# Four instead of five plain experts in a one-core attention–MoE–FFN kernel, with the extra VectorE work tied to the side product's remainder

## The chip, the cores and the metric

The kernel runs on one core of one Trainium2 chip. The metric is the device time of one execution in microseconds. The five engines run their own instruction streams: TensorE (PE), VectorE (DVE), ScalarE (ACT), GpSimd (POOL), and SyncE (SP), which here issues the DMAs. An instruction waits for others through semaphores, and everything behind it on its own engine waits with it.

## The reference

Three layers follow each other. Attention takes the 32 largest scores of each row (2 batches, 8 heads, 576 rows, head size 64). Its output is x, 1152 rows of 512. The mixture of experts and the last layer are

```python
logits = x @ w_gate
P = np.exp(logits - logits.max())
for _ in range(8):
    P /= P.sum(1, keepdims=True) + 1e-09
    P /= P.sum(0, keepdims=True) + 1e-09
    P *= N / E
for e in range(E):                       # E = 8, F = 1024
    h = np.maximum(x @ w1[e], 0.0)
    out += P[:, e:e + 1] * (h @ w2[e])

h = out @ w_in                           # 512 x 2048
g = h * np.tanh(np.log1p(np.exp(h)))     # h itself above 20
result = g @ w_out                       # 2048 x 512
```

Every product is made to float32 accuracy from pairs of rounded numbers (a high part, and a low part that is the remainder), three matmuls for one. The last layer's weights come as the bits of float64.

## The kernel before

**Stages.** The 1152 rows are nine tiles of 128. The experts run in three chunks of rows: tiles 0 and 1, tiles 2 and 3 (both beside attention), and tiles 4 to 8, which is 640 rows, from about 559 to 994 us. Then comes the last layer ("d" in names), in two units of four and five tiles, to the end at 1196 us. This case is about the third chunk ("c2") and its seam to the last layer.

**Plain experts.** The weights of an expert come in eight pieces of 128 hidden columns. Experts 0 to PLAIN - 1 run piece by piece (`ffn_pass`). A piece has 24 first-layer matmuls (L805) and 15 of the second layer (L679). ACT writes the high part of the activation (`hh`, L633) and DVE the remainder (`hl`, L634).

**Seven products.** The other experts take two pieces at a time (`pair_pass`): the first layer of the pair is a 2x2 block product, done with seven products instead of eight (42 matmuls of 320 columns at L711). The banks `run` and `alt` (two of them in all) and one side bank `hs` take them in the order 11, side product 12, s2, s3 and s1, 22, s4; second-layer matmuls of the pair before stand in between, as groups of 6 and 9. DVE's part of a pair is written in `total` and `Relu.first`: `hs` becomes a total (L729) and gives a remainder (L634); `c` becomes a total (L729) and gives one; `run` gives one; `h` becomes a total and gives one. PE's s4 waits for the `c` total, because it writes the bank that the total reads, and the next pair's product 11 waits for the remainder of `run` for the same reason.

**Weights.** `load_pair` makes the weight sums on POOL (L569 to L573), ACT rounds each (`wh`, L542), and POOL subtracts (`wl`, L546). For the third chunk the raw pieces come from the weights; for "d" they come from a DRAM copy `w` that the kernel itself has made (next paragraph), into tiles `wraw_d` and `wrawb_d`.

**Work that fills the third chunk.** On DVE: 32 *doubles*, each a 128x512 block of float64 weights turned into float32 by one ACT square and six DVE operations (L954, L957 to L961), loaded by SP into `cx` and stored by SP (L962) from `cb` to `w`; 32 *rows*, in which a spilled second-layer output is read back and added (L826); and 24 *lefts* (L618 add or subtract, L619 cast, L620 subtract), the operand sums for seven products in the last layer's first unit. On POOL: 32 *sums*, the same three lines for the operand of the third chunk. The buffers of the doubles live in pool `cp`; when the doubles are done (`conv.close()`), pool `x2q`, which holds `wraw_d` and `wrawb_d`, takes the same memory.

**What sets the order.** PE's order is that of the program. On the other engines a priority by stream decides, except where `after(a, b)` says that a comes behind b. `pace` hangs doubles and rows behind the newest remainder `live["hl"]`, at rates in pieces (`DOUBLES`, `FILL_FROM`); `follow` gives lefts a credit and hangs one behind its second argument for each whole credit. In the loop over the third chunk's yields, `TURN_FROM`, `PAIRS_FROM` and `TURNS` say at which of them a tile of the finished output is transposed (`x2t`, L985), which the lefts need.

```python
pieces += 1 if pieces < PLAIN * EP else 2 / 3
pace(pieces)
if i >= TURN_FROM and (i - PAIRS_FROM) % 8 in TURNS:
    next(first_rows, None)
```

## Time and profile before

| | us |
|---|---|
| median of 3 runs (lowest to highest) | 1195.77 (1195.69 to 1196.48) |
| the profiled execution | 1198.0 |
| its span, first to last instruction | 1196.1 |
| PE busy | 1150.1 (96%) |
| DVE, ACT, POOL busy | 926.4, 712.8, 704.3 |

The span is the profiler's, of one execution, from the first instruction to the last. Busy time is the time in which an engine had an instruction in work, and an engine that is waited for can be far from fully busy. The mean granted TensorE clock is 0.994 of full speed.

### The profile page before, as it was taken

To read this page: it belongs to the slowest core of one execution; us is meant where nothing else is said; L and a number is where in the kernel's file an instruction comes from. 1 tells how busy PE (TensorE), PEld (TensorE's weight loads), DVE (VectorE), ACT (ScalarE), POOL (GpSimd) and SP (SyncE) were. 2 spreads that over 40 slices of the span, in tenths; PEclk is the share of its full clock that TensorE was granted. 3 is DMA by queue.
4 is the path that set the end of the run, shared out by engine and by line. 5 is a ranking of instruction groups with operands and counts; after the bars stand their busy time and mean duration, and the time that the engine had idled before them with its cause. 6 is when DMAs were issued, how large, how long until landed. Compare 5 with 4: busy or idle time off the path is not lost.

```text
span 1196.1 us, 21441 instructions
## 1 busy us (share of the span) xinstructions
PE 1150.1 (96%) x7251; PEld 1025.3 (86%) x7251; DVE 926.4 (77%) x1943; ACT 712.8 (60%) x1454; POOL 704.3 (59%) x607
## 2 busy tenths in 40 slices
PE   3788999999999999999999999999999999999998
PEld 2566888898888999889999999998898989889997
DVE  7999999999999999943578888777666457886442
ACT  5877777777777777754233333333455546767653
POOL 6544877888777787762223343433665576787651
PEclk9998999999999999999999999999999999999999
DMA  8358777657565677754257776766454332233201
GB/s 254 106 180 280 237 258 232 187 162 226 177 214 169 214 235 231 242 174 158 81 175 246 247 256 222 268 209 229 164 177 141 125 114 80 97 107 115 96 29 45
DMA packets 121967, 214.08 MB, mean 179 GB/s; under 512 B 16000, under 2 KB 26496, under 8 KB 121856
## 3 DMA queue, kind: packets, MB, share of 16 engines
q1 hardware_dynamic: 120560, 211.52, 54.5%
q8 instruction: 57, 0.93, 0.3%
q10 hardware_dynamic: 1296, 1.18, 0.3%
q14 instruction: 54, 0.44, 0.1%
HBM read 174.11 MB, written 38.54 MB: 178 GB/s over the span
## 4 chain that ended last, share of the span: by engine, by line
PE 87%; DVE 3%; DMA 1%; ACT 1%; issue 1%; POOL 0%; SPq 0%; ACTq 0%; POOLq 0%
PE y_c2e L679 17%; PE h_c2e L805 11%; PE y_d L679 8%; PE h_c1e L805 8%; PE y_c1e L679 8%; PE h_c0e L805 6%; PE y_c0e L679 6%; PE h_d L711 6%; PE h_c2e L711 5%; PE pv L358 3%; PE tr L335 2%; PE sc L236 2%; PE pv L365 1%; PE hs_d L711 1%; PE hs_c2e L711 1%
## 5 line engine op out<-in xcount | busy, mean ns | idle before, releaser
L546 POOL TENSOR_TENSOR wl_c1e<-wraw_c1e,wh_c1e 128x512 fp32r<-128x512 f32 x128 | 171.2, 1348 | 60.2 <-ACT wh_c1e L542 56.9
L546 POOL TENSOR_TENSOR wl_c0e<-wraw_c0e,wh_c0e 128x512 fp32r<-128x512 f32 x112 | 148.3, 1337 | 51.1 <-ACT wh_c0e L542 44.1
L264 DVE MAX8 top<-w 128x8 f32<-128x576 f32 x216 | 158.5, 748 | 1.0
L546 POOL TENSOR_TENSOR wl_c2e<-wraw_c2e,wh_c2e 128x512 fp32r<-128x512 f32 x40 | 53.2, 1330 | 171.6 <-ACT wh_c2e L542 163.7
L542 ACT ACTIVATE wh_c2e<-wraw_c2e 128x512 fp32r<-128x512 f32 x80 | 50.6, 632 | 143.6 <-PE y_c2e L679 76.9
L542 ACT ACTIVATE wh_c1e<-wraw_c1e 128x512 fp32r<-128x512 f32 x128 | 80.5, 629 | 47.3 <-PE y_c1e L679 22.1
L271 DVE MATCH_REPLACE8 w<-top,w 128x576 f32<-128x576 f32 x144 | 106.6, 741 | 0.0
L805 PE MATMUL h_c2e<-xh,wh_c2e 128*128 128x256 f32 (+1 forms) x320 | 98.7, 308 | 0.6 <-DVE hl_c2e L634 0.6
L805 PE MATMUL h_c2e<-xl,wh_c2e 128*128 128x256 f32 (+1 forms) x320 | 98.2, 307 | 0.0
L805 PE MATMUL h_c2e<-xh,wl_c2e 128*128 128x256 f32 (+1 forms) x320 | 98.1, 307 | 0.0
L542 ACT ACTIVATE wh_c0e<-wraw_c0e 128x512 fp32r<-128x512 f32 x112 | 70.4, 629 | 46.1 <-PE y_c0e L679 15.6
L634 DVE SCALAR_TENSOR_TENSOR hl_c2e<-h_c2e,hh_c2e 128x256 fp32r<-128x256 f32 (+1 forms) x104 | 50.6, 487 | 53.8 <-ACT hh_c2e L633 53.6
L236 PE MATMUL sc<-ks,q 128*128 128x288 f32 x320 | 66.0, 338 | 23.6 <-POOL ks L168 5.5
L236 PEld LDWEIGHTS sc<-ks,q 128*128 128x128 f32 x320 | 53.1, 211 | 34.1 <-ACT early L249 7.4
L679 PE MATMUL y_c2e<-wh_c2e,hl_c2e 128*128 128x512 f32 x200 | 78.7, 394 | 0.0
L679 PE MATMUL y_c2e<-wl_c2e,hh_c2e 128*128 128x512 f32 x200 | 78.4, 392 | 0.0
L679 PE MATMUL y_c2e<-wh_c2e,hh_c2e 128*128 128x512 f32 x200 | 78.4, 392 | 0.0
L805 PE MATMUL h_c1e<-xh,wh_c1e 128*128 128x256 f32 (+1 forms) x256 | 76.4, 298 | 0.0
L665 DVE TENSOR_TENSOR hl_d<-mg_d,hh_d 128x256 fp32r<-128x256 f32 (+1 forms) x64 | 50.5, 796 | 32.4 <-ACT hh_d L664 32.0
L805 PE MATMUL h_c1e<-xh,wl_c1e 128*128 128x256 f32 (+1 forms) x256 | 73.3, 286 | 0.0
L805 PE MATMUL h_c1e<-xl,wh_c1e 128*128 128x256 f32 (+1 forms) x256 | 73.2, 286 | 0.0
L805 PE MATMUL h_c0e<-xh,wh_c0e 128*128 128x256 f32 x224 | 66.7, 298 | 1.1 <-DVE hl_c0e L634 0.9
(532 smaller groups left out, 3963.0 us busy)
## 6 DMA issues: line engine op xcount, KB each, us to landing
wraw_c1e<-in_wst_dram SPq DMA_DIRECT2D x128, 256.0 KB, 3.1
wraw_c0e<-in_wst_dram SPq DMA_DIRECT2D x112, 256.0 KB, 3.2
wraw_c2e<-in_wst_dram SPq DMA_DIRECT2D x80, 256.0 KB, 3.3
cx<-in_w_dram SPq DMA_DIRECT2D x32, 512.0 KB, 5.0
yd<-ysp SPq DMA_DIRECT2D x32, 256.0 KB, 3.6
low<-wl_c1e SPq DMA_DIRECT2D x32, 256.0 KB, 2.7
yb<-yd SPq DMA_DIRECT2D x32, 256.0 KB, 3.6
wl_c2e<-low SPq DMA_DIRECT2D x32, 256.0 KB, 3.8
```

The costliest lines, as they stand in the source:

```text
L236: nc.tensor.matmul(halves[half], q[:, h % HG, :], ks[b, h][:, half * HS : (half + 1) * HS], start=(i == 0), stop=(i == len(terms) - 1),)
L264: top8 = nc.vector.max(g, src)
L271: nc.vector.match_replace(w, g, src, NEG)
L335: nc.tensor.transpose(tr[:, c, :], em[:, j * D + c * P :][:, :P], ident)
L358: nc.tensor.matmul(pv[i * D : (i + 1) * D, pair, c0:c1], vmain[b, pair][:, i, c, :], live["at", i][:, c, c0:c1], start=(c == 0), stop=False,)
L542: live["rounded"] = nc.scalar.activation(hi, raw, AF.Copy)
L546: eng.tensor_sub(lo, raw, hi)
L634: live["hl"] = nc.vector.scalar_tensor_tensor(l, ps, 0.0, h, op0=ALU.max, op1=ALU.subtract)
L665: follow(LEFT_RATE, nc.vector.tensor_sub(l, g, h))
L679: nc.tensor.matmul(y, h[:, j * P : (j + 1) * P], w, start=(start and k == 0), stop=(stop and k == len(products) - 1))
L711: nc.tensor.matmul(bank, a[:, cols], b[:, c, :], start=(start and c + k == 0), stop=(c == 1 and k == 2), skip_group_check=not start,)
L805: nc.tensor.matmul(ps, w[:, c * P : (c + 1) * P], x[:, c, c0 : c0 + m], start=(k == 0), stop=(k == 3 * NC - 1),)
```

## The change

One expert more (expert 4) runs by seven products: `PLAIN` is 4. The yields are counted anew (`PAIRS_FROM`, `TURN_FROM`), and the transposes are at two of three places (`TURNS[:2]`). The paces of rows, doubles and sums become tables of a start and a rate. In the experts by seven products the doubles and the lefts no longer hang behind whatever remainder came last. They hang behind the remainder of the side product (`live["lead"]`), in every pair but an expert's first, 2.7 lefts and one double for each such pair; `follow` is gone from `Relu` and, in the third chunk, from the totals. The combine of the last second-layer outputs is ordered behind a remainder (`put_last`).

```diff
--- before.py
+++ after.py
@@ -48,10 +48,10 @@
 EARLY_FROM, EARLY_STEPS = 5, 9
 HOLD, RATE = 8, 0.25
 ALONE, ALONE_RATE = 1, 3.4
-FILL_FROM = 9
-PLAIN = 5
-PAIRS_FROM, TURN_FROM = 78, 126
-DOUBLES, LEFT_RATE, SUMS = (7, 0.8, 0.4), 0.4, (7, 1.15)
+PLAIN = 4
+PAIRS_FROM, TURN_FROM = 62, 78
+ROWS, DOUBLES, SUMS = ((8, 1.25),), ((7, 0.8), (32, 0.375)), ((7, 1.4),)
+LEFT_RATE, LEFT_PAIR = 0.4, 2.7
 KEPT = ((1, 2, 3), (4, 5, 6, 7))
 TURNS = (2, 4, 6)
 
@@ -632,8 +632,6 @@
             h, l = self.hh[:, c0 : c0 + m], self.hl[:, c0 : c0 + m]
             nc.scalar.activation(h, ps, AF.Relu)
             live["hl"] = nc.vector.scalar_tensor_tensor(l, ps, 0.0, h, op0=ALU.max, op1=ALU.subtract)
-            if carry:
-                follow(LEFT_RATE, live["hl"])
 
     class LateRelu(Relu):
 
@@ -726,7 +724,9 @@
         def total(bank, u, act, half, last=True):
             with st("first"):
                 c = bank if last else tp.tile([P, m], F32, tag="c", name=f"c_{tag}_{g}", bufs=2)
-                follow(1, nc.vector.tensor_add(c, bank, u))
+                added = nc.vector.tensor_add(c, bank, u)
+                if tag[0] == "d":
+                    follow(1, added)
                 act.first(c, half * m, m)
 
         def carried():
@@ -747,6 +747,9 @@
             side = ps_b.tile([P, 512], F32, tag="misc", name=f"hs_{tag}_{g}")[:, :m]
             product(side, "12", "21", True)
             total(side, p1, acts[0], 0)
+            if tag[0] == "c" and g:
+                live["lead"] = live["hl"]
+                follow(LEFT_PAIR, live["hl"])
             yield
             yield from carried()
             product(run, "s2", "t2", False)
@@ -865,7 +868,7 @@
             )
 
     def put_last(e, t, y):
-        combine(t, e, y)
+        after(combine(t, e, y), live["hl"])
 
     def handed_over(tiles):
         while pending:
@@ -1004,15 +1007,19 @@
     paced = {"rows": [], "doubles": []}
     held = dict.fromkeys(paced, 0)
 
-    def pace(n):
-
-        first, rate, later = DOUBLES
-        due = (min(n, PLAIN * EP) - first) * rate + max(n - PLAIN * EP, 0) * later
-        for kind, ahead in (("rows", n - FILL_FROM + 1), ("doubles", due + 1)):
-            for group in paced[kind][held[kind] : max(int(ahead), 0)]:
-                for inst in group:
-                    after(inst, live["hl"])
-                held[kind] += 1
+    def due(plan, n):
+
+        ends = [at for at, _ in plan[1:]] + [n]
+        return sum(max(min(n, end) - at, 0) * rate for (at, rate), end in zip(plan, ends))
+
+    def pace(n, inst):
+
+        for kind, plan in (("rows", ROWS), ("doubles", DOUBLES)):
+            if n >= plan[0][0]:
+                for group in paced[kind][held[kind] : int(due(plan, n)) + 1]:
+                    for each in group:
+                        after(each, inst)
+                    held[kind] += 1
 
     def once_gated():
 
@@ -1036,14 +1043,15 @@
     last, pieces, drawn = live["hl"], 0, 0
     for i, _ in enumerate(moe_chunk(len(CHUNKS) - 1)):
         next(gating, None)
-        if live["hl"] is not last:
-            last = live["hl"]
-            pieces += 1 if pieces < PLAIN * EP else 2 / 3
-            pace(pieces)
-            while sums and drawn < (pieces - SUMS[0]) * SUMS[1]:
+        mark = live["hl"] if pieces < PLAIN * EP else live.get("lead", last)
+        if mark is not last:
+            last = mark
+            pieces += 1 if pieces < PLAIN * EP else 8 / 3
+            pace(pieces, last)
+            while sums and drawn < due(SUMS, pieces):
                 after(sums.pop(0), last)
                 drawn += 1
-        if i >= TURN_FROM and (i - PAIRS_FROM) % 8 in TURNS:
+        if i >= TURN_FROM and (i - PAIRS_FROM) % 8 in TURNS[:2]:
             next(first_rows, None)
     for _ in first_rows:
         pass
```

In the changed kernel the lines from L942 on are numbered three higher (the conversion is L957, L960 to L964, the store L965), the totals are L727 instead of L729, and a combine is L829 instead of L826.

On DVE, in the third pair of expert 5, the rows before were (`hs` is the side product's bank, `c` the alternate one's total, `hl` a remainder):

```order
L729 TENSOR_TENSOR hs_c2e_2_11551<-hs_c2e_2_11551,p_c2e_2_11549 128x320
L634 SCALAR_TENSOR_TENSOR hl_c2e_4_11538<-hs_c2e_2_11551,hh_c2e_4_11537 128x320
L954 TENSOR_SCALAR cb_0_9224<-cx_0_9221 128x512
L957 SCALAR_TENSOR_TENSOR ca_0_9223<-cx_0_9221,cb_0_9224 128x512
L958 TENSOR_SCALAR cb_0_9224<-ca_0_9223 128x512
L959 SCALAR_TENSOR_TENSOR cb_0_9224<-cx_0_9221,cb_0_9224 128x512
L960 TENSOR_TENSOR cb_0_9224<-ca_0_9223,cb_0_9224 128x512
L961 SCALAR_TENSOR_TENSOR cb_0_9224<-cd_0_9225,cb_0_9224 128x512
L729 TENSOR_TENSOR c_c2e_2_11598<-h_c2e_2_1_11542,u_c2e_2_11590 128x320
L634 SCALAR_TENSOR_TENSOR hl_c2e_5_11540<-c_c2e_2_11598,hh_c2e_5_11539 128x320
```

and with the change:

```order
L727 TENSOR_TENSOR hs_c2e_2_11678<-hs_c2e_2_11678,p_c2e_2_11676 128x320
L634 SCALAR_TENSOR_TENSOR hl_c2e_4_11665<-hs_c2e_2_11678,hh_c2e_4_11664 128x320
L620 TENSOR_TENSOR t_d_11396<-x_0_11095,t_d_11396 128x256
L957 TENSOR_SCALAR cb_0_9170<-cx_0_9167 128x512
L618 TENSOR_TENSOR x_0_11095<-x_0_11095 128x256
L960 SCALAR_TENSOR_TENSOR ca_0_9169<-cx_0_9167,cb_0_9170 128x512
L619 CAST t_d_11397<-x_0_11095 128x256
L961 TENSOR_SCALAR cb_0_9170<-ca_0_9169 128x512
L962 SCALAR_TENSOR_TENSOR cb_0_9170<-cx_0_9167,cb_0_9170 128x512
L963 TENSOR_TENSOR cb_0_9170<-ca_0_9169,cb_0_9170 128x512
L964 SCALAR_TENSOR_TENSOR cb_0_9170<-cd_0_9171,cb_0_9170 128x512
L727 TENSOR_TENSOR c_c2e_2_11725<-h_c2e_2_1_11669,u_c2e_2_11717 128x320
```

Two or three lefts (L618 to L620) have come in among the six conversions, between the side product's remainder and the `c` total. The same stands in eight pairs, those of experts 5 to 7 but their first. In three of the eight the last of the six conversions stands behind the `c` total, as in the last pair of expert 7, whose double is the 32nd and last:

```order
L634 SCALAR_TENSOR_TENSOR hl_c2e_6_12891<-hs_c2e_3_12904,hh_c2e_6_12890 128x320
L618 TENSOR_TENSOR x_0_11095<-x_0_11095 128x256
L957 TENSOR_SCALAR cb_1_9264<-cx_1_9261 128x512
L619 CAST t_d_11399<-x_0_11095 128x256
L960 SCALAR_TENSOR_TENSOR ca_1_9263<-cx_1_9261,cb_1_9264 128x512
L620 TENSOR_TENSOR t_d_11399<-x_0_11095,t_d_11399 128x256
L961 TENSOR_SCALAR cb_1_9264<-ca_1_9263 128x512
L962 SCALAR_TENSOR_TENSOR cb_1_9264<-cx_1_9261,cb_1_9264 128x512
L546 TENSOR_TENSOR wl_d_0b<-wraw_d_0b,wh_d_0b 128x512
L963 TENSOR_TENSOR cb_1_9264<-ca_1_9263,cb_1_9264 128x512
L727 TENSOR_TENSOR c_c2e_3_12951<-h_c2e_3_1_12895,u_c2e_3_12943 128x320
L964 SCALAR_TENSOR_TENSOR cb_1_9264<-cd_1_9265,cb_1_9264 128x512
```

(`hs_c2e_3` is the side bank of the fourth pair; `wl_d` are weights of the last layer.)

On SP, where the stores of the last double (`w_15<-cb_1`) and the loads for the last layer stand, the rows before were, among the loads of expert 6:

```order
L533 DMA wraw_c2e_0b<-in_wst_dram 128x512
L533 DMA wraw_c2e_0a<-in_wst_dram 128x512
L962 DMA w_15_9247<-cb_1_9264 128x512
L533 DMA wrawb_d_0b<-w_1_8869 128x512
L533 DMA wrawb_d_1b<-w_3_8923 128x512
L544 DMA wl_c2e_3b<-low_7_7173 128x512
L533 DMA wraw_c2e_1a<-in_wst_dram 128x512
```

and with the change:

```order
L533 DMA wraw_d_1a<-w_2_8896 128x512
L965 DMA w_15_9247<-cb_0_9251 128x512
L533 DMA wraw_d_1a<-w_2_8896 128x512
L533 DMA wraw_d_1b<-w_3_8923 128x512
L533 DMA wraw_d_2a<-w_4_8950 128x512 x2
L965 DMA w_15_9247<-cb_1_9264 128x512
L533 DMA wrawb_d_0b<-w_1_8869 128x512
L533 DMA wrawb_d_1b<-w_3_8923 128x512
L533 DMA wraw_d_2b<-w_5_8977 128x512
```

The load of `wrawb_d_0b` stands right behind the store of the 32nd double in both. In the changed kernel that double is the one in expert 7's last pair, and the rows behind it are loads of the last layer.

## Rows read from the trace of the kernel before

**Rows 1.** The page, parts 1 and 4: busy time; the chain that ended last

```profile
PE 1150.1 (96%) x7251; PEld 1025.3 (86%) x7251; DVE 926.4 (77%) x1943; ACT 712.8 (60%) x1454; POOL 704.3 (59%) x607
...
PE 87%; DVE 3%; DMA 1%; ACT 1%; issue 1%; POOL 0%; SPq 0%; ACTq 0%; POOLq 0%
```

**Rows 2.** Windows, experts 4 and 5: length, busy by engine, clock, DMA, GB/s

```profile
778.77:834.80 56.03, 55.46 (x314) 50.15 (x312) 42.46 (x67) 19.38 (x38) 19.25 (x18) 1.00 0.67 223
834.80:887.09 52.29, 52.29 (x289) 47.16 (x288) 35.50 (x53) 26.70 (x54) 31.55 (x28) 1.00 0.54 174
```

**Rows 3.** Timeline of DVE, a pair of expert 5: start, length, instruction, idle before

```profile
864.39 1.34 DVE L954 TENSOR_SCALAR cb<-cx 128x512 uint32<-128x512 uint32 x1
...
868.94 0.69 DVE L960 TENSOR_TENSOR cb<-ca,cb 128x512 f32<-128x512 f32 x1
869.74 1.59 DVE L961 SCALAR_TENSOR_TENSOR cb<-cd,cb 128x512 f32<-128x512 f32 x1
871.25 0.48 DVE L729 TENSOR_TENSOR c_c2e<-h_c2e,u_c2e 128x320 f32<-128x320 f32 x1
...
873.11 0.49 DVE L634 SCALAR_TENSOR_TENSOR hl_c2e<-h_c2e,hh_c2e 128x320 fp32r<-128x320 f32 x1 [0.35 <-ACT hh_c2e L633]
```

**Rows 4.** Timeline of PE: the next pair's first product

```profile
874.00 0.31 PE L711 MATMUL h_c2e<-xh,wh_c2e 128*128 128x320 f32 x1
```

**Rows 5.** Timeline of DVE: the next pair

```profile
877.44 0.42 DVE L954 TENSOR_SCALAR cb<-cx 128x512 uint32<-128x512 uint32 x1
877.89 0.69 DVE L957 SCALAR_TENSOR_TENSOR ca<-cx,cb 128x512 uint32<-128x512 uint32 x1
878.62 0.43 DVE L958 TENSOR_SCALAR cb<-ca 128x512 uint32<-128x512 uint32 x1
...
882.97 0.48 DVE L729 TENSOR_TENSOR c_c2e<-h_c2e,u_c2e 128x320 f32<-128x320 f32 x1
```

**Rows 6.** Timeline of POOL beside rows 3

```profile
864.15 1.30 POOL L546 TENSOR_TENSOR wl_c2e<-wraw_c2e_3a,wh_c2e 128x512 fp32r<-128x512 f32 x1
...
869.15 1.63 POOL L546 TENSOR_TENSOR wl_c2e_s<-ws_c2e,wh_c2e_s 128x512 fp32r<-128x512 f32 x1 [0.79 <-ACT wh_c2e_s L542]
```

**Rows 7.** Timelines of DVE and POOL: a left beside a weight product

```profile
950.25 1.25 DVE L620 TENSOR_TENSOR t_d<-x,t_d 128x256 fp32r<-128x256 f32 x1
...
949.92 1.30 POOL L546 TENSOR_TENSOR wl_c2e_s<-ws_c2e,wh_c2e_s 128x512 fp32r<-128x512 f32 x1 [0.79 <-ACT wh_c2e_s L542]
```

**Rows 8.** Timeline of PE: a transpose in expert 6

```profile
917.75 0.44 PE L985 MATMUL x2t<-ident,acc 128*128 128x128 f32 x2 [0.32 <-DVE hl_c2e L634]
```

**Rows 9.** Timeline of SP's queue: last store, first load behind it

```profile
917.32 0.33 SPq L962 DMA_DIRECT2D w<-cb  x1
919.38 0.33 SPq L533 DMA_DIRECT2D wrawb_d_0b<-w  x1
```

**Rows 10.** DMAs: issues, size, median us from issue to landing

```profile
wrawb_d_0b<-w SPq DMA_DIRECT2D x2, 256.0 KB, 2.6
```

**Rows 11.** Timeline of DVE: the c total of expert 7's last pair

```profile
989.33 0.49 DVE L729 TENSOR_TENSOR c_c2e<-h_c2e,u_c2e 128x320 f32<-128x320 f32 x1 [0.47 <-ACT wh_d_s L542]
```

**Rows 12.** Timelines of POOL and ACT: weight sums of the last layer

```profile
984.11 0.74 POOL L570 TENSOR_TENSOR wrawb_d_1b<-wrawb_d_1b 128x256 f32<-128x256 f32 x1
...
989.41 1.30 POOL L546 TENSOR_TENSOR wl_d_s<-ws_d,wh_d_s 128x512 fp32r<-128x512 f32 x1 [1.62 <-ACT wh_d_s L542]
...
988.71 0.62 ACT L542 ACTIVATE wh_d_s<-ws_d 128x512 fp32r<-128x512 f32 x1
```

**Rows 13.** Timeline of PE: the last layer's s2

```profile
997.27 0.28 PE L711 MATMUL h_d<-t_d,wl_d_s 128*128 128x256 f32 x1
```

**Rows 14.** Timeline of PE in attention: a wait

```profile
114.10 0.48 PE L358 MATMUL pv<-at,vm 128*64 128x128 f32 x2 [2.73 <-ACT at L349]
```

**Rows 15.** Windows in attention (columns as in rows 2)

```profile
62.20:65.60 3.40, 3.38 (x22) 2.63 (x21) 3.40 (x9) 2.47 (x6) 0.00 (x0) 0.50 0.76 253
...
113.40:120.20 6.80, 6.10 (x35) 5.80 (x36) 6.50 (x19) 2.83 (x7) 3.46 (x3) 0.50 0.92 321
```


## The prediction, written before the changed kernel ran

> **What bounds the kernel now.** I read the page first. PE is busy for 96% of the span, and 87% of the chain that ended last is PE [rows 1]. So the time is PE's own work, and a change counts in two ways only: it removes matmuls, or it makes PE wait. The second view is the windows of two neighbouring experts of the third chunk [rows 2]: PE is busy for 55.46 of 56.03 us in plain expert 4 and for all of 52.29 us in expert 5, at a clock of 1.00. The third is the timelines of DVE and POOL inside one pair, where one sees how close the extra VectorE work already comes to the point at which PE would wait [rows 3 to 6]. The last are SP's queue and the seam between expert 7 and the last layer [rows 9 to 13], since the changed order moves the last conversion there.
>
> **The change part by part.**
>
> *Expert 4 by seven products (A).* Its PE work falls from 55.46 to 52.29 us [rows 2], 3.17 less. Where the plain expert lost its 0.57 us of idling, the remaining plain ones have the same loads and the same doubles ahead of them, so I let that stall stay. A = **-3.2**. POOL has 31.55 us of work in such an expert instead of 19.25, and ACT 26.70 instead of 19.38 [rows 2]. Both are far below 52, so they cost nothing by their sums.
>
> *Paces in the plain experts, the combine of the last outputs.* The rows and sums come somewhat faster. In the plain expert DVE was busy for 42.46 of 56 us [rows 2], and that spare 13.6 us covers them; if the cover is gone, a late remainder stops PE as the 0.57 us did. Taken as 0.
>
> *Transposes moved.* One waited 0.32 us for a remainder in expert 6 [rows 8]. In the changed order another, in expert 4, stands behind a double in the same way. One goes and one comes: 0.
>
> *Lefts inside the pairs (S).* The block that hangs behind the side product's remainder must be through before PE needs the `c` total, because the `c` total, its remainder and that of `run` follow it on DVE, and the next pair's product 11 waits for the last of these. In the pair of [rows 3], the block starts at 864.39 and the total follows at 871.25. The remainder ends at 873.60 (873.11 + 0.49), and PE starts the next pair at 874.00 without a wait [rows 4]. So the total could come 0.40 later, at 871.65, and the block may take 7.26 us. A lone double took 6.86 there, and 5.53 in the next pair (877.44 to 882.97) [rows 5]. The room is 0.40 or 1.73 us. Now two or three lefts come in. One beside a POOL product took 1.25 us: POOL ended at 951.22, the left at 951.50 [rows 7]. So a left that has to sit out POOL's instruction has 0.28 us of its own left over behind it. Three such add some 0.7 to 0.8 if they fall into stretches that DVE loses to POOL anyway, and up to 3 us if not. Against 0.40 of room, 0.3 to 0.8 us is over; against 1.73, nothing. Half of the eight pairs at 0.55 makes S = **+2.2**. The bounds are 0 (all fit) and 8 (1.0 in each of the eight).
>
> *The last layer's first load (D).* SP takes its DMAs in order, and `wrawb_d_0b` uses the memory that the last double gives up. Before, the store of that double was issued at 917.32 and the load at 919.38 [rows 9], some 75 us before the last layer needs it. In the changed order the last double is converted in expert 7's last pair. In the clock of the trace of before: the `c` total there starts at 989.33 [rows 11], and the last conversion is behind it, so it ends no sooner than 989.82 + 0.69 (its shortest neighbour, rows 3) = 990.5. The step from store to load was 2.06 us, so the load goes at 992.6 and lands 2.6 later [rows 10], at 995.2. POOL has four sums in its order up to `ws_d_0`, 0.74 each [rows 12]: 998.2. ACT rounds in 0.62: 998.8. POOL has three more sums, to 1000.4, then the product `wl_d_s`, 1.30 [rows 12]: 1001.7. PE needed it at 997.27 [rows 13]. That is 4.4 late if nothing else is; D = **+4.5**. The ends are 0 (if the load is not held) and 7 (if DVE reaches the last conversion 2.5 us later, three lefts and a weight product of the last layer being in that block).
>
> *What follows a wait of PE (K).* In the whole trace after 122 us no wait of PE is longer than 1 us, so this case is bounded from attention. There a wait of 2.73 us [rows 14] was followed by 6.8 us at a granted clock of 0.50 (1.2 instead of 2.4 GHz), and a stretch with many small waits by 3.4 us at 0.50 [rows 15]. Half of these is lost: 3.4 or 1.7. The wait at the seam would come in two parts with matmuls between, in a stretch otherwise dense, so I take the smaller: K = **+1.7**, ends 0 and 3.4.
>
> **The sum.** -3.2 + 0 + 0 + 2.2 + 4.5 + 1.7 = **+5.2 us**. The profiled execution took 1198.0, which is 2.2 above the median of the runs (1195.77); it would become 1203.2, and the median **1201.0**.
>
> *A rule against the rows.* In [rows 6] POOL works from 864.15 to 870.78 but for 0.79 us, 5.6 of it inside DVE's block of 6.86. The six conversions by themselves need at least 0.42 + 0.69 + 0.43 [rows 5] and three times 0.69, which is 3.6. Together 9.2, so the two engines did work at the same time for 2.3 us. The Trainium skill ("SBUF — State Buffer", section "Who interferes with whom") says that a VectorE operation with two SBUF inputs and a GpSimd operation that reads SBUF share a port pair under an exclusive lock, and that the loser blocks for the whole instruction. The trace agrees for single instructions, as the left above, which ended just behind POOL's. Taken for the whole block the rule would make S about 23 (fourth rival).
>
> **The rivals.**
>
> 1. *The blocks fit, and the small stalls go.* S = 0, and the 0.57 and 0.32 us of idling [rows 2, 8] go with the new paces; D = 4.4 without a fall of the clock. -3.2 - 0.9 + 4.4 = +0.3: **1196.1**, no change. For it: the next pair's double had 1.73 to spare. Against it: three lefts ask for up to 3. Chance 0.17.
> 2. *The other side: the load is not held.* One mechanism decides it: whether the last conversion is through early enough. If DVE gets to it before about 986 in the old clock, which is 4.4 earlier than worked out above, `wl_d_s` is there in time, D and K vanish, and with fitting blocks only A is left: **1192.6**, faster. Against it stands the order on DVE, where the conversion is behind the `c` total, and that needs `alt`, which PE writes only shortly before. Chance 0.10.
> 3. *The seam costs its upper ends.* D = 7 and K = 3.4: -3.2 + 2.2 + 7 + 3.4 = +9.4, **1205.2**. For it: the lefts in that block, and the one comparable wait [rows 14]. Chance 0.16.
> 4. *DVE and POOL exclude each other in the blocks.* 9.2 for a double and POOL, and three lefts of about 0.35 (half the columns of a 0.69 operation, an estimate) make 10.2, so 2.9 over in eight pairs, 23 in all: **about 1222**. The 2.3 us of overlap speak against it. Chance 0.02.
>
> The forecast keeps 0.55.
>
> **How the numbers follow.** Two per mille, 2.4 us, is about what a measurement of this kernel can tell from no change. Below 1193.4 lies rival 2: faster 0.10. Rival 1 lies within: same 0.17. The forecast and rivals 3 and 4 lie above 1198.2: slower 0.73. The range goes from 1195.0, which takes in rival 1, to 1206.0, which takes in rival 3 and S at twice its value; it leaves out rivals 2 and 4 and the far tails, under 0.2 together.
>
> **What would show it.** In the changed profile, PE's first s2 of the last layer waits for ACT's `wh_d_s` or POOL's `wl_d_s`, 4 us or more in all, and SP issues `wrawb_d_0b` only after expert 7's last `c` total. The granted clock falls behind that. In the pairs of experts 5 to 7 PE waits for a DVE remainder or total, 0.3 to 0.8 us in about half of them. An expert 4 of 52.3 us shows A. The forecast is wrong if that load is issued well before the last pair, if PE has no wait at the seam, or if the waits in the pairs add up to over 5 us.

## The result: slower by 0.63%, and where the time is in the profile after

| | before | after |
|---|---|---|
| median of 6 runs, us | 1196.12 | 1204.22 |
| ratio after / before | | 1.0063 (95% interval 1.0048 to 1.0078) |
| the profiled execution, us | 1198.0 | 1203.92 |
| its span, us | 1196.1 | 1202.1 |

One of the six runs after took 1652.85 us at a mean granted clock of 0.655 and is left out of the ratio; the median of the other five is 1203.92.

The rows of the page after that answer to [rows 1]:

```profile
PE 1148.7 (96%) x7227; PEld 1022.3 (85%) x7227; DVE 943.9 (79%) x1955; ACT 721.9 (60%) x1474; POOL 727.8 (61%) x631
...
PE 84%; DVE 5%; ACT 1%; DMA 1%; issue 1%; POOL 1%; SPq 0%; ACTq 0%; DVEq 0%; POOLq 0%
```

PE's busy time is 1.4 us less than before (with the slower stretch that is shown below in it), and the share of PE in the chain has gone down from 87% to 84%, that of DVE up from 3% to 5%. So the seven products did take work from PE, and PE waits longer. Where it waits is shown by windows cut at the first matmul of a side product: the plain experts of the third chunk, the experts by seven products, the seam (first to second side product of the last layer), and the rest. The columns are those of [rows 2]. Before:

```profile
559.45:835.68 276.23, 275.66 (x1576) 251.14 (x1575) 207.09 (x375) 96.82 (x191) 92.13 (x79) 1.00 0.66 216
835.68:994.98 159.30, 158.98 (x883) 142.91 (x881) 94.64 (x161) 82.55 (x168) 97.68 (x96) 1.00 0.43 140
994.98:1006.71 11.73, 11.73 (x74) 10.50 (x73) 8.74 (x15) 8.36 (x17) 7.53 (x9) 1.00 0.27 87
1006.71:1192.07 185.36, 184.88 (x1078) 165.54 (x1076) 112.96 (x172) 119.31 (x268) 114.47 (x110) 1.00 0.24 80
```

After:

```profile
558.27:778.46 220.19, 220.19 (x1264) 200.99 (x1263) 170.88 (x315) 77.24 (x153) 80.43 (x71) 1.00 0.66 218
778.46:994.21 215.75, 212.85 (x1170) 190.06 (x1169) 150.92 (x234) 108.97 (x223) 124.41 (x118) 1.00 0.48 156
994.21:1013.34 19.13, 14.03 (x74) 11.86 (x73) 7.49 (x14) 10.02 (x20) 15.53 (x18) 0.82 0.18 59
1013.34:1198.52 185.18, 185.09 (x1078) 165.58 (x1076) 110.40 (x172) 119.23 (x268) 114.69 (x110) 1.00 0.24 80
```

The plain experts are 56.04 us shorter, and the experts by seven products 56.45 us longer, so that an expert less by eight products has brought nothing: they took 215.75 instead of the 212 or so that four such experts need without waits. The seam took 19.13 instead of 11.73 us, 7.40 more. The rest is the same within 0.2. Together this is +7.6. The two spans are only 6.0 apart, because the third chunk began 1.2 us earlier in this execution of the changed kernel than in that of before, which is attention's part, and the stretch behind the last window was 0.4 shorter.

**The seam.** PE's timeline has two waits there:

```profile
999.70 0.79 PE L709 MATMUL h_d<-t_d,wh_d_s 128*128 128x256 f32 x2 [3.27 <-ACT wh_d_s L542]
1002.33 0.58 PE L709 MATMUL h_d<-t_d,wl_d_s 128*128 128x256 f32 x1 [1.83 <-POOL wl_d_s L546]
```

They are 3.27 + 1.83 = 5.10 us. The chain behind them, on DVE, SP and POOL in order of time:

```profile
988.61 0.49 DVE L727 TENSOR_TENSOR c_c2e<-h_c2e,u_c2e 128x320 f32<-128x320 f32 x1
989.01 0.69 DVE L964 SCALAR_TENSOR_TENSOR cb<-cd,cb 128x512 f32<-128x512 f32 x1
...
989.73 0.32 SPq L965 DMA_DIRECT2D w<-cb  x1
991.78 0.32 SPq L533 DMA_DIRECT2D wrawb_d_0b<-w  x1
992.15 0.42 SPq L533 DMA_DIRECT2D wrawb_d_1b<-w  x1
...
994.57 0.74 POOL L569 TENSOR_TENSOR ws_d<-wraw_d_0a,wrawb_d_0b 128x256 f32<-128x256 f32 x1 [10.27 <-DMA wrawb_d_0b<-w]
996.64 0.72 POOL L569 TENSOR_TENSOR ws_d<-wraw_d_1a,wrawb_d_1b 128x256 f32<-128x256 f32 x1 [1.33 <-DMA wrawb_d_1b<-w]
...
1001.00 1.27 POOL L546 TENSOR_TENSOR wl_d_s<-ws_d,wh_d_s 128x512 fp32r<-128x512 f32 x1
```

The last conversion (L964) comes right behind the `c` total and ends at 989.70. SP issues its store, and 2.05 us later the load of `wrawb_d_0b`, at 991.78; POOL's first sum can begin at 994.57. This is the sequence that was worked out ahead, within a microsecond at each step up to POOL's first sum (store to load 2.06, landing 2.6, [rows 9, 10]). One link was not in it: the second sum in POOL's order needs `wrawb_d_1b`, which SP issued 0.37 later and which landed at 996.5, so POOL stood another 1.33 us. Then the clock:

```profile
996.40:1002.40 6.00, 0.90 (x4) 0.57 (x3) 0.42 (x1) 2.91 (x7) 5.76 (x8) 0.69 0.00 1
1002.40:1005.00 2.60, 2.60 (x8) 2.27 (x9) 0.00 (x0) 0.38 (x1) 2.60 (x3) 0.50 0.11 36
```

The granted clock fell within the first wait, in which PE did nothing, and is at 0.50 (1.2 GHz) from there until about 1005; an s2 matmul takes 0.58 instead of 0.28 us [rows 13].

Where the 7.40 us come from can be told by the first product with `wl_d_s`, which is the last that was late. In the kernel before, it started 2.29 us after the side product (997.27 and 994.98), with the change 8.12 us (1002.33 and 994.21): late data cost 5.83. From there to the next side product PE had no wait, and took 11.01 instead of 9.44 us: the lower clock cost 1.57.

**The pairs.** In the changed kernel's experts 5 to 7, the pairs with lefts and a double were these. There are nine of them, all but each expert's first; the eight of the section on the change is a miscount. "Block" is the time from the first instruction behind the side product's remainder (0.41 us after that starts) to the start of the `c` total, "c total" its start after that of the side product, and "lost" the pair's length (side product to side product) over the usual 13.06 us:

| expert, pair | lefts, conversion steps ahead of c | block | c total | lost |
|---|---|---|---|---|
| 5, second | 2, 6 | 7.41 | 10.28 | 0.62 |
| 5, third | 3, 6 | 8.62 | 11.18 | 1.52 |
| 5, fourth | 3, 6 | 9.00 | 11.56 | 1.90 |
| 6, second | 2, 5 | 7.29 | 10.16 | 0.50 |
| 6, third | 3, 6 | 7.24 | 9.80 | 0.14 |
| 6, fourth | 3, 6 | 7.26 | 9.81 | 0.14 |
| 7, second | 3, 5 | 7.09 | 9.97 | 0.30 |
| 7, third | 2, 6 | 6.37 | 8.94 | 0.00 |
| 7, fourth | 3, 5 | 4.43 | 7.30 | 0.00 |

(The last pair ends at the seam and is 12.90 long, as in e7, which has no double there.) The losses sum to 5.12 us; the timeline, in which the ends of matmuls are modelled, shows 2.90 of them as waits of PE. In every row that lost, they are the start of the `c` total less 9.66 us: the slack that [rows 3, 4] gave (the total at 871.25, 0.40 of room, the side product at 861.83: 9.82) is right to 0.16, and what comes later than that is lost one for one. What fills a block is seen in expert 5's third pair. DVE:

```profile
861.83 0.81 DVE L620 TENSOR_TENSOR t_d<-x,t_d 128x256 fp32r<-128x256 f32 x1
862.57 1.52 DVE L957 TENSOR_SCALAR cb<-cx 128x512 uint32<-128x512 uint32 x1
864.00 0.96 DVE L618 TENSOR_TENSOR x<-x 128x256 f32<-128x256 f32 x1
864.88 1.23 DVE L960 SCALAR_TENSOR_TENSOR ca<-cx,cb 128x512 uint32<-128x512 uint32 x1
866.03 0.83 DVE L619 CAST t_d<-x 128x256 fp32r<-128x256 f32 x1
866.78 1.51 DVE L961 TENSOR_SCALAR cb<-ca 128x512 uint32<-128x512 uint32 x1
868.33 0.69 DVE L962 SCALAR_TENSOR_TENSOR cb<-cx,cb 128x512 f32<-128x512 uint32 x1
869.06 0.69 DVE L963 TENSOR_TENSOR cb<-ca,cb 128x512 f32<-128x512 f32 x1
869.85 0.69 DVE L964 SCALAR_TENSOR_TENSOR cb<-cd,cb 128x512 f32<-128x512 f32 x1
870.46 0.48 DVE L727 TENSOR_TENSOR c_c2e<-h_c2e,u_c2e 128x320 f32<-128x320 f32 x1
```

and POOL beside it:

```profile
861.61 0.76 POOL L569 TENSOR_TENSOR ws_c2e<-wraw_c2e_3a,wraw_c2e_3b 128x256 f32<-128x256 f32 x1 [2.16 <-DMA wraw_c2e_3b<-in_wst_dram]
862.32 1.49 POOL L546 TENSOR_TENSOR wl_c2e<-wraw_c2e_3a,wh_c2e 128x512 fp32r<-128x512 f32 x1
863.76 0.92 POOL L570 TENSOR_TENSOR wraw_c2e_3b<-wraw_c2e_3b 128x256 f32<-128x256 f32 x1
864.64 0.92 POOL L571 TENSOR_TENSOR ws_c2e<-wraw_c2e_3b,ws_c2e 128x256 f32<-128x256 f32 x1
865.64 1.07 POOL L573 TENSOR_TENSOR wraw_c2e_3a<-wraw_c2e_3a,ws_c2e 128x256 f32<-128x256 f32 x1
866.67 1.34 POOL L546 TENSOR_TENSOR wl_c2e_s<-ws_c2e,wh_c2e_s 128x512 fp32r<-128x512 f32 x1
```

POOL's six instructions end at 862.37, 863.81, 864.68, 865.56, 866.71 and 868.01. DVE's first six end at 862.64, 864.09, 864.96, 866.11, 866.86 and 868.29: 0.15 to 0.55 behind each of them. In this block DVE gets one instruction through for each of POOL's: a left of half the columns takes 0.81 to 0.96, and a step that takes 0.42 alone [rows 5] takes 1.52. Only the last three run at their own 0.69. PE feels the end of it in the next pair's first product:

```profile
872.87 0.41 PE L709 MATMUL h_c2e<-xh,wh_c2e 128*128 128x320 f32 x1 [0.73 <-DVE hl_c2e L634]
```

The Trainium skill ("SBUF — State Buffer", section "Who interferes with whom") has VectorE and GpSimd take a shared port pair for a whole instruction, by order of issue. Instructions that let each other pass in turn agree with that.

### The profile page after: what moved, and what is told of

It reads as the page before. It is cut to its first block, busy times and chain, and to the rows that moved or that the text cites. A ratio compares the mean times of both kernels' runs of the same rounds, so it can differ in the third digit from the quotient of the medians.

```text
span 1202.1 us, 21467 instructions
## 1 busy us (share of the span) xinstructions
PE 1148.7 (96%) x7227; PEld 1022.3 (85%) x7227; DVE 943.9 (79%) x1955; ACT 721.9 (60%) x1474; POOL 727.8 (61%) x631
## 4 chain that ended last, share of the span: by engine, by line
PE 84%; DVE 5%; ACT 1%; DMA 1%; issue 1%; POOL 1%; SPq 0%; ACTq 0%; DVEq 0%; POOLq 0%
PE y_c2e L677 16%; PE h_c2e L808 9%; PE y_d L677 8%; PE h_c1e L808 8%; PE y_c1e L677 8%; PE h_c0e L808 6%; PE h_d L709 6%; PE y_c0e L677 6%; PE h_c2e L709 5%; PE pv L358 3%; PE tr L335 2%; PE sc L236 2%; PE pv L365 1%; PE hs_c2e L709 1%; PE hs_d L709 1%
## 5 line engine op out<-in xcount | busy, mean ns | idle before, releaser
L546 POOL TENSOR_TENSOR wl_c2e<-wraw_c2e,wh_c2e 128x512 fp32r<-128x512 f32 x32 | 42.5, 1327 | 132.1 <-ACT wh_c2e L542 124.8
L542 ACT ACTIVATE wh_c2e<-wraw_c2e 128x512 fp32r<-128x512 f32 x64 | 40.5, 633 | 114.7 <-PE y_c2e L677 60.4
L634 DVE SCALAR_TENSOR_TENSOR hl_c2e<-h_c2e,hh_c2e 128x256 fp32r<-128x256 f32 (+1 forms) x96 | 46.8, 488 | 45.1 <-ACT hh_c2e L633 45.0
L808 PE MATMUL h_c2e<-xh,wh_c2e 128*128 128x256 f32 (+1 forms) x256 | 78.9, 308 | 0.0
L808 PE MATMUL h_c2e<-xl,wh_c2e 128*128 128x256 f32 (+1 forms) x256 | 78.6, 307 | 0.0
L808 PE MATMUL h_c2e<-xh,wl_c2e 128*128 128x256 f32 (+1 forms) x256 | 78.5, 307 | 0.0
L663 DVE TENSOR_TENSOR hl_d<-mg_d,hh_d 128x256 fp32r<-128x256 f32 (+1 forms) x64 | 45.6, 718 | 33.1 <-ACT hh_d L662 32.7
L677 PE MATMUL y_c2e<-wh_c2e,hl_c2e 128*128 128x512 f32 x160 | 63.0, 394 | 0.0
L677 PE MATMUL y_c2e<-wh_c2e,hh_c2e 128*128 128x512 f32 x160 | 62.8, 393 | 0.0
L808 PE MATMUL h_c0e<-xh,wl_c0e 128*128 128x256 f32 x224 | 62.8, 280 | 0.0
```

The source lines that it names most:

```text
L542: live["rounded"] = nc.scalar.activation(hi, raw, AF.Copy)
L546: eng.tensor_sub(lo, raw, hi)
L634: live["hl"] = nc.vector.scalar_tensor_tensor(l, ps, 0.0, h, op0=ALU.max, op1=ALU.subtract)
L663: follow(LEFT_RATE, nc.vector.tensor_sub(l, g, h))
L677: nc.tensor.matmul(y, h[:, j * P : (j + 1) * P], w, start=(start and k == 0), stop=(stop and k == len(products) - 1))
L808: nc.tensor.matmul(ps, w[:, c * P : (c + 1) * P], x[:, c, c0 : c0 + m], start=(k == 0), stop=(k == 3 * NC - 1),)
```

## The experiments

All are kernels of one core, timed in rounds against the kernel before on the same chip. "Sevens" and "seam" are the second and third windows as above, from the profiled execution.

| | median us | ratio to before (95%) | sevens | seam |
|---|---|---|---|---|
| before | 1196.12 to 1197.0 | 1 | 159.30 (3 experts) | 11.73 |
| the change | 1204.22 | 1.0063 (1.0048 to 1.0078) | 215.75 | 19.13 |
| e1 last double a pair earlier | 1199.99 | 1.0027 (1.0016 to 1.0037) | 218.30 | 11.90 |
| e2 first loads in other memory | 1202.88 | 1.0055 (1.0036 to 1.0073) | 219.92 | 12.78 |
| e3 lefts spread as before | 1200.51 | 1.0033 (1.0021 to 1.0045) | 212.89 | 18.85 |
| e4 before, last double late | 1202.81 | 1.0056 (1.0044 to 1.0067) | 158.48 (3 experts) | 19.69 |
| e5 before with PLAIN 4 | 1198.68 | 1.0017 (1.0008 to 1.0025) | 216.10 | 11.89 |
| e6 lefts spread, last double earlier | 1194.56 | 0.9979 (0.9971 to 0.9988) | 211.79 | 11.73 |
| e7 lefts behind the pair's end | 1193.32 | 0.9973 (0.9964 to 0.9982) | 212.02 | 11.74 |
| e8 seam filled with matmuls | 1204.59 | 1.0064 (1.0052 to 1.0077) | 217.74 | 16.44 |
| e9 one conversion step in two | 1202.14 | 1.0045 (1.0031 to 1.0058) | 220.43 | 11.90 |

Four experts by seven products without any wait would have some 211 to 212 in "sevens": sixteen pairs of 13.06 and 1.8 for the sixteen transposes that stand in them; the two shortest measured are 211.79 and 212.02. Each kernel has one profiled execution, so the windows are of that one, and the medians are of five to eleven runs.

### e4: the kernel before, with its last double late

```diff
+            if tag == "c2e7" and g == 3:
+                live["tail"] = live["hl"]
...
-        for kind, ahead in (("rows", n - FILL_FROM + 1), ("doubles", due + 1)):
+        for kind, ahead in (("rows", n - FILL_FROM + 1), ("doubles", min(due + 1, 31))):
...
+    for inst in paced["doubles"][31]:
+        after(inst, live["tail"])
```

> The kernel before with one edit: its 32nd double hangs behind the side product's remainder in expert 7's last pair. Theory: the seam alone is reproduced, waits of 4 to 5 us and the lower clock behind them, 1196.1 + 6 to 7.4 = 1202 to 1203.5, nothing else moves. Rival (the seam's wait needs the other changes too, the lefts or POOL's new order): within 1 us of 1196.1.

Measured: 1202.81 us, ratio 1.0056.

```profile
834.25:992.73 158.48, 158.48 (x883) 143.07 (x882) 92.28 (x161) 80.94 (x165) 88.55 (x86) 1.00 0.43 137
992.73:1012.42 19.69, 14.78 (x75) 12.46 (x73) 7.93 (x15) 10.01 (x20) 15.27 (x18) 0.83 0.24 81
```

The seam is 19.69 at a mean clock of 0.83, and the pairs are as before. The theory's numbers are met. One double in the wrong place costs the kernel before 6 us, with five plain experts and its own lefts, so nothing else of the change is needed for the seam's wait.

### e1: the last double one pair earlier

```diff
-ROWS, DOUBLES, SUMS = ((8, 1.25),), ((7, 0.8), (32, 0.375)), ((7, 1.4),)
+ROWS, DOUBLES, SUMS = ((8, 1.25),), ((7, 0.8), (32, 0.38)), ((7, 1.4),)
```

> The changed kernel with the second rate of the doubles at 0.38 instead of 0.375: each double from expert 4's fourth pair on comes one pair earlier, and the last is converted in expert 7's third pair instead of its fourth. Theory (the seam's wait is the load of wrawb_d_0b, held by the last conversion): the load goes some 12 us earlier, PE's two waits at the seam (3.27 and 1.83 us) and the fall of the clock behind them go, side product of d0 to that of d1 takes 11.7 us instead of 19.1, the time is 1196.8 (7.4 less), pair stalls as they were. Rival (POOL and ACT have too much to do at the seam, the load is not what is late): the waits stay over 3 us and the time over 1201.

Measured: 1199.99 us, 4.2 under the change, not 7.4.

```profile
779.15:997.45 218.30, 213.77 (x1170) 189.92 (x1169) 158.65 (x234) 109.86 (x226) 133.26 (x128) 1.00 0.49 155
997.45:1009.35 11.90, 11.90 (x75) 10.59 (x73) 7.88 (x14) 8.37 (x17) 7.75 (x9) 1.00 0.29 92
```

The seam is back at 11.90 with no wait, as the theory has it, and the rival is out. But "sevens" is 2.55 longer. Part of it is the double that came into expert 4's fourth pair, beside the transposes (the pair took 14.52 instead of 13.97). Most is in pairs whose order on DVE did not change: expert 6's third and fourth and expert 7's third took 1.2 to 1.3 more each, and expert 5's fourth 1.90 less. Expert 6's third pair in the change, with DVE's block from the first left to the `c` total, and POOL's first instruction:

```profile
918.00 0.28 DVE L619 CAST t_d<-x 128x256 fp32r<-128x256 f32 x1
...
925.24 0.48 DVE L727 TENSOR_TENSOR c_c2e<-h_c2e,u_c2e 128x320 f32<-128x320 f32 x1
...
919.10 0.80 POOL L569 TENSOR_TENSOR ws_c2e<-wraw_c2e_3a,wraw_c2e_3b 128x256 f32<-128x256 f32 x1 [3.48 <-DMA wraw_c2e_3b<-in_wst_dram]
```

and in e1:

```profile
917.41 0.28 DVE L619 CAST t_d<-x 128x256 fp32r<-128x256 f32 x1
...
925.98 0.48 DVE L727 TENSOR_TENSOR c_c2e<-h_c2e,u_c2e 128x320 f32<-128x320 f32 x1
...
917.90 0.75 POOL L569 TENSOR_TENSOR ws_c2e<-wraw_c2e_3a,wraw_c2e_3b 128x256 f32<-128x256 f32 x1 [2.88 <-DMA wraw_c2e_3b<-in_wst_dram]
```

With three lefts and six steps in both, the block is 7.24 us in the one and 8.57 in the other. POOL's first sum waits for a load, and began 1.10 us after the block did in the change, 0.49 in e1. In the first, four of DVE's nine instructions have begun before POOL starts and cost what they cost alone; in the second two have. So "pair stalls as they were" was wrong: with full blocks a small shift of POOL against DVE is worth 1.3 us in a pair. What shifts the load was not tried.

### e2: the first loads in other memory

```diff
-        if own and "x2q" in live:
+        if own and "x2q" in live and tag not in ("d0_0b", "d0_1b"):
```

> The changed kernel, but the two first second-operand loads of the last layer (d_0b, d_1b) take buffers of the other raw weights and not the memory that the doubles give up; the last double stays in expert 7's last pair. Theory (the reused memory is the link between the last conversion and the load): as without the hold, d0 to d1 11.7 us, the time 1196.8. Rival (the late conversion itself, or its store ahead on SP's queue, is enough): waits at the seam over 3 us, the time over 1201.

Measured: 1202.88 us. The miss is in the time, not in the link:

```profile
778.62:998.54 219.92, 214.21 (x1171) 189.88 (x1169) 156.60 (x233) 109.52 (x226) 129.83 (x125) 1.00 0.48 151
998.54:1011.32 12.78, 12.16 (x75) 10.64 (x74) 6.02 (x12) 7.70 (x16) 7.71 (x10) 1.00 0.40 124
```

```profile
983.55 0.32 SPq L533 DMA_DIRECT2D wraw_d_0b<-w  x1
...
996.43 0.32 SPq L965 DMA_DIRECT2D w<-cb  x1
```

The load (it is called `wraw_d_0b` here) is issued 12.9 us before the last double's store, and PE's waits for `wh_d_s` and `wl_d_s` are gone: the reused memory is the link, and a late conversion alone does not stop PE at the seam. What was gained went elsewhere. "Sevens" is 4.2 longer: two pairs of expert 6 took 14.50 and 14.58 us instead of 13.20, full blocks as in e1, and expert 7's last took 14.32 instead of 12.90, since POOL's sums for the last layer, no longer late, now run beside the last double's block. The seam is 1.05 longer than before, and the rest 1.5 longer than in the change. The last layer's loads have fewer buffers in this kernel, and PE waited 0.62 and 1.08 us for ACT in its first pairs; that this comes from the buffers was not tried.

### e3: the lefts spread as before

```diff
             live["hl"] = nc.vector.scalar_tensor_tensor(...)
+            if carry:
+                follow(LEFT_RATE, live["hl"])
...
-                if tag[0] == "d":
-                    follow(1, added)
+                follow(1, added)
...
                 live["lead"] = live["hl"]
-                follow(LEFT_PAIR, live["hl"])
```

> The changed kernel, but the lefts hang behind remainders and totals by the credit of the kernel before, not 2.7 behind the side product's remainder; doubles and all else as changed. Theory (the lefts are what overfills the blocks of expert 5): PE's waits in the pairs of experts 5 to 7 fall from about 5 us to under 1.5, the seam stays as it is, the time is 1200.5. Rival (a double beside POOL's sums overfills the pair alone, lefts or no lefts): the waits stay at 4 to 5 us, the time at 1204.

Measured: 1200.51 us.

```profile
778.53:991.42 212.89, 211.93 (x1171) 190.24 (x1169) 152.32 (x234) 108.81 (x223) 128.09 (x118) 1.00 0.51 158
```

"Sevens" is 2.86 shorter than with the change, and the seam is still there at 18.85. PE's waits in experts 5 to 7 are 0.9 us in all, where the timeline of the change has 2.9; by the lengths of the pairs the loss is 2.2 instead of 5.1. The time is the theory's. So the lefts are what overfills most of the blocks, some 2.9 of the 5.1. The other 2.2 are lost in pairs with a double and one left or none, so doubles are not free of it. e3 removes one cause and leaves the other, and e1 does the reverse; whether the two add is what e6 asks.

### e6 and e7: both causes removed

e6 is e3 with e1's rate. e7 is e1's rate with the lefts moved behind the `c` total:

```diff
-                follow(LEFT_PAIR, live["hl"])
...
                 acts[1].first(run, 0, m)
+                if tag[0] == "c":
+                    follow(LEFT_PAIR, live["hl"])          # LEFT_PAIR is 2.0 here
```

> The lefts spread as in e3 and the doubles' rate of e1 together. Theory (two causes that add): e3's time less the seam, 1200.5 - 7.1 = 1193.4, with up to 1 us for the double that comes into expert 4's fourth pair: 1194, faster than both. Rival (what the seam gives is given back in the pairs, as in e1): 1196.5 or more.

> The changed kernel with the doubles' rate of e1, and two lefts in every pair behind the remainder of the run bank, after the c total, in place of 2.7 before it. Theory (what counts is the DVE work between the side product's remainder and the c total, which must come by 9.66 us after the side product's start): blocks of a lone double of 5.5 to 7.5 us, waits in the pairs under 1.5 us in all, no seam: 1194. Rival (lefts are as dear anywhere in a pair, since DVE is short of time there): waits of 4 us or more, 1198.

Measured: 1194.56 and 1193.32 us. Both beat the kernel before (0.9979 and 0.9973, both intervals below 1). Of e7:

```profile
777.01:989.03 212.02, 211.38 (x1170) 190.11 (x1169) 157.75 (x234) 110.08 (x226) 136.65 (x128) 1.00 0.50 160
```

The DVE work is no less than in the change (157.75 us in this window against 150.92). What differs is that no left stands between the side product's remainder and the `c` total. The blocks of a double alone took 5.1 to 7.5 us. This decides between the two theories of e7: it is that one interval that is short, not DVE.

### e5: the kernel before with four plain experts

```diff
-PLAIN = 5
-PAIRS_FROM, TURN_FROM = 78, 126
-DOUBLES, LEFT_RATE, SUMS = (7, 0.8, 0.4), 0.4, (7, 1.15)
+PLAIN = 4
+PAIRS_FROM, TURN_FROM = 62, 142
+DOUBLES, LEFT_RATE, SUMS = (7, 0.8, 0.4), 0.4, (7, 1.4)
```

> The kernel before with four plain experts alone: PLAIN 4, the yields counted anew so that the transposes stay in expert 6's third pair, and POOL's sums at 1.4 a piece so that they are ready for expert 4; doubles, rows and lefts hang as before. Its last double is in expert 7's third pair. Theory: expert 4 gives 3.2 to 3.8, nothing is late at the seam, and lone doubles stop PE by 1 to 2 us in all: 1194.5. Rival (the eight-to-seven gain is eaten in the pairs whatever is hung behind what): 1197 or more.

Measured: 1198.68 us, past the rival's bound (1197), and slightly slower than before (1.0008 to 1.0025). The seam has no wait (11.89). "Sevens" is 216.10, some 4 too long, and not by lefts ahead of the `c` total. Its longest pairs are those with transposes (15.45 us), two (14.98 and 14.21) in which outputs of an expert are added and a double begun between the remainder of `c` and that of `run`, where PE waits 1.62 and 0.87 us for the latter, and the one behind the first of these (14.30), where the rest of that double holds the remainder of `h`, and PE waits 0.96. So the fourth expert by seven products does not pay with the old placing either; e6 and e7 show that it pays with doubles behind the side product and lefts elsewhere.

### e8: the seam's wait filled with matmuls

```diff
+            if tag == "d0" and g == 0:
+                for _ in range(5):
+                    product(alt, "11", "11", True)
             product(run, "s2", "t2", False)
```

> The changed kernel with 30 matmuls of product 11 made again into the alternate bank, just ahead of the last layer's first s2; s1 overwrites them. They take 3.5 us of PE in a wait of 5.1. Theory (the clock fell because PE stood still): the granted clock stays at 1.00 behind the seam, the side product of d0 to that of d1 takes 16.8 us instead of 19.1, the time is 1202. Rival (the fall has another cause, or the wait moves with the added work): 19 us or more, 1204 or more.

Measured: 1204.59 us, no gain. The window of the seam says more:

```profile
779.63:997.37 217.74, 213.37 (x1171) 190.05 (x1170) 151.42 (x233) 108.30 (x223) 124.41 (x118) 1.00 0.48 153
997.37:1013.81 16.44, 15.58 (x104) 14.11 (x103) 7.46 (x12) 10.03 (x20) 15.25 (x17) 1.00 0.21 67
```

The mean clock of the seam is 1.00, and it takes 16.44 instead of 19.13, 2.7 less with 30 matmuls more. So the fall does come from PE's standing still. Not all of the 2.7 is the clock's:

```profile
998.56 0.74 POOL L569 TENSOR_TENSOR ws_d<-wraw_d_1a,wrawb_d_1b 128x256 f32<-128x256 f32 x1 [0.15 <-POOL ws_d L569]
1004.25 0.38 PE L709 MATMUL h_d<-t_d,wl_d_s 128*128 128x256 f32 x1 [0.86 <-POOL wl_d_s L546]
```

POOL's second sum waited 0.15 us and not 1.33, since `wrawb_d_1b` landed 3.1 us after its issue instead of 4.3, and the first product with `wl_d_s` came 6.88 us after the side product instead of 8.12. That is 1.24 of it. From there to the next side product PE took 9.56 instead of 11.01 us, so the fall cost 1.5 in the change. The same stretch took 12.02 in e4 and 12.23 in e3, against 9.44 before: there it cost 2.6 and 2.8.

The time did not follow. In that execution "sevens" was 2.0 longer by the blocks described under e1, and the third chunk began 1.2 later; whether the other runs lost their gain in the same way is not shown. The edit lies behind "sevens", and the instructions in it stand in the same order on DVE, ACT and POOL as in the change, so the 2.0 come from no edit: the pairs of experts 5 to 7 lost 7.1 us here and 5.1 in the change. The total alone would have told the opposite.

### e9: one step of the conversion cut in two

```diff
-        begin = nc.vector.tensor_scalar(p2, top, 3, 0x3FFFFFFF, ...)
+        cuts = (0, 256, 512) if len(paced["doubles"]) >= 21 else (0, 512)
+        begins = [nc.vector.tensor_scalar(p2[:, i:j], top[:, i:j], 3, 0x3FFFFFFF, ...) for i, j in zip(cuts, cuts[1:])]
```

> e1 with one edit: the first of the six conversion operations is cut into two of 256 columns in the doubles of the experts by seven products; the elements are the same, each block has one instruction more. Theory (beside POOL's work DVE gets one instruction through for each of POOL's, so instructions count and not elements): a block with three lefts grows from 8.55 us by one full operation that is left over behind POOL's work, to about 9.2, a pair that lost 1.44 loses about 2.1, blocks of doubles alone grow by 0.4 to 0.7, and the time is 3 to 5 us above e1's 1200.0. Rival (elements count): the blocks grow by under 0.1 us, the time stays within 1 us of 1200.0.

Measured: 1202.14 us, 2.15 above e1, between the two. The blocks that were full in both, expert 5's third and expert 6's fourth, grew from 8.56 and 8.55 to 8.86 and 8.87, by 0.3 rather than 0.7. Two others moved much more and against each other, expert 5's fourth from 6.70 to 8.72 and expert 6's third from 8.57 to 7.31, by the shift described under e1, so the 2.15 us of the time are not the cut's alone. In expert 5's third pair the two halves took 2.15 us together beside two of POOL's instructions, where the whole step had taken 1.52 beside one; but the first left had begun before POOL did, which it had not in e1, and that gave part of it back. The same elements in one instruction more cost three times what the rival allowed (under 0.1). The size of one slot stays unsettled by this run.

## Why the prediction was right, step by step

The forecast was +5.2 us, 1201.0; measured were +8.1 and 1204.2. The way and the range were right, but the range, 1195.0 to 1206.0, is wider than the effect and took in no change as well, so that it held says little of the terms. By its steps:

- **A, expert 4 by seven products: -3.2.** Right. Expert 4 took 54.08 us (side product to side product, four pairs), of which 1.8 are the transposes: 52.3. The 0.57 us of idling in the plain expert, which I had let stay, went too (220.19 of 220.19 us busy), so this part gave 3.8.
- **Transposes: 0.** They gave 0.5. Before, the two pairs with transposes were 2.3 us longer than others, after 1.8.
- **S, lefts in the pairs: +2.2.** The mechanism was right, and the size was off: 5.1 in the profiled execution, and 7.1 in that of e8, whose order there is the same. From "a left that has to sit out POOL's instruction has 0.28 us of its own left over" I concluded that three add 0.7 to 0.8. The 0.28 is met in the pair shown; the step that failed is the condition behind it, that lefts fall into stretches that DVE loses to POOL anyway. A left does not only add its tail. It takes the place beside one of POOL's instructions, and the conversion step that would have had that place runs later at its full length. Expert 5's third pair, 0.3 to 0.8 over by my working, was 1.52 over, and the fourth 1.90. Expert 6's third and fourth, where POOL began later, were 0.14 over. "Half of the eight pairs" was wrong too: there are nine, and seven lost. The limit was right to 0.16 as a time after the side product, but it is no fixed length of the block: in an expert's second pair the block starts 0.3 later, and 7.09 was already 0.30 over.
- **D, the held load: +4.5.** Measured 5.8, by the time at which `wl_d_s` came. The step from conversion to store to load to sums held with its numbers; e4 made it alone and e2 removed the link alone. What lacked is `wrawb_d_1b`, for which POOL waited 1.33 more.
- **K, the clock: +1.7.** Measured 1.6, as what the stretch behind the last late product took more. (PE's busy time in the seam grew by 2.3, but the part of it between the two waits only shortened the second wait.) e8 confirms the cause. The size is partly luck: it was 2.6 and 2.8 in e4 and e3.

The terms as measured make -3.8 - 0.5 + 5.1 + 5.8 + 1.6 = +8.2; the windows gave +7.6 and the medians +8.1. Of what the forecast lacked, 2.9 are S.

Of the forecast's own signs of being wrong, the first two did not come: the load was issued after the last `c` total, and PE had its waits at the seam. The third, waits in the pairs of over 5 us, is met by the lost lengths (5.12) and not by the waits that the timeline shows (2.90); it points at S, as the terms do.

Of the rivals, the first (blocks that fit) fails by the 5.1 us. The second (load not held) fails by the seam. The third had its number nearest, 1205.2, but for another reason: it put D at 7 and K at 3.4, and S at 2.2 only. The fourth (full exclusion) is wrong in size: the block of 8.62 has 6.2 us of POOL's work in it, so 2.4 are left for nine DVE instructions that need more than 4. But its idea was nearer to the truth than the forecast's price of a left: the two engines take turns.

## What to carry to other kernels

When work is put into a gap of an engine that another one holds up, as POOL does DVE here, count its instructions too, and not only its microseconds: in expert 5's third pair six of nine each took a turn of the other engine's length, though e9 found less than a full turn for one more. Find which interval is short (here between the side product's remainder and the `c` total) and hang the extra work behind it, not into it. And when memory is handed from one pool to the next, look for the last user of the old one: moving it late holds the first loads of the new one, with everything behind them on the queue, however early these stand in the program.

## What the runs showed that was not expected

The same nine instructions in the same order took 7.24 us or 8.57 us in a pair, by whether POOL started 1.10 or 0.49 us behind them, and 1.3 us per pair went to PE one for one. This moved "sevens" from 215.75 in the change to 217.74 in e8, which differs only behind it. With one profile for each kernel, it stays open whether such a shift belongs to a kernel or to an execution. A step of 0.42 us on one operand of 128x512 (L957) took 1.52 beside POOL, so it is not only operations on two operands that wait.
